# Windowed attention into a two-layer expert network: the first pair's weight splits moved to VectorE and earlier, a one-hot product moved to VectorE, a shorter unused path on ScalarE

## The chip, the cores and the metric

One core of a Trainium2 chip runs the whole program. The metric is device time in microseconds of that core, lower is better; the time shown for a kernel is the median of its runs. The engines are TensorE (PE, its weight loads PEld), VectorE (DVE), ScalarE (ACT), GpSimd (POOL) and SyncE (SP, which issues most DMAs); a "q" behind a name is that engine's instruction queue.

## The reference

```python
scores = scale * q @ k.T                     # B, H, S, D = 4, 8, 768, 64
keep = is_sink | in_window                   # 4 sinks, a window of 128
a = exp(where(keep, scores, -1e9) - max); a = a / (sum(a) + 1e-9)
x = (a @ v) as (3072, 512)
logits = x @ w_gate + modality_bias[modality_id]        # 8 experts
e_idx = argmax(logits); gate_w = softmax(logits)[e_idx]
for e in experts:
    out[e_idx == e] = gate_w * (relu(x[e_idx == e] @ w1[e]) @ w2[e])   # 512 -> 1024 -> 512
h = out @ w_in; out = (h * sigmoid(1.702 * h)) @ w_out  # 512 -> 2048 -> 512
```

All of it is float32. The kernel multiplies float32 numbers as two parts, a rounded one and the rest ("split": `exact()` writes the rounded part on ScalarE, and subtracts it from the number on a second engine, L1095 and L1096).

## The kernel before, in words

The program has four stages. **Start** (0 to 16 us): constants, the loads of the first tiles, and a branch at L1045 on whether window and sinks are of the size that the fast path handles. The path not taken, `general()`, stands in every engine's program between the branch and what follows it, so each engine jumps over its own part of it. **Attention** (to about 217 us): 24 tiles of 128 tokens. Each kind of step of a tile (`scores`, `mask`, `expo`, `ptrans`, `pevac`, `pv`, `back`, `norm` and more) has a time in the table `AT`, counted in quarters of a tile; all steps of all tiles are sorted by these times and written out in that order, which is each engine's order. The tables `OPEN` (the opening of the next stage) and `MORE` (the search for the first expert, and the loads of its weights) put further steps into the same order.

**Routing and the first pair of token blocks** (to about 257 us): the first pair's expert is chosen from the first 16 tiles, so its 256 tokens are gathered (L1016), scaled (L1116), transposed (L1107, `x0` and `x1`) and put through the expert while the attention ends. The expert's weights are 8 chunks of 512 KB (`raw0` to `raw7`, L1072 and L1073); each is split into `wah` and `wal` (128 x 1024). `first(0, f)` multiplies by chunk f's first weight (L1143, 12 matmuls, "up") and leaves relu's two parts (L1166 on ScalarE, L1169 on VectorE); `down_pair(0, f)` multiplies by its second (L1158, 12 matmuls, "down"). Beside that runs `route()`, a generator of some 45 small VectorE steps: the last tile's one-hot `pk_oh` (L649), two products on TensorE (L802, L803), then the places of all tokens, the one-hot matrices `r_es` (L908), `r_bt` (L910) and `r_at` (L914, four pieces), 24 products on TensorE (L917), and `perm` (L926), by which GpSimd gathers the second pair's tokens. The table `ADV` says how many of these steps are written inside and behind each chunk f. **The rest** (to 1091 us): 14 further pairs, single blocks, then the dense layers.

Before the change three chunks' subtractions (0, 1, 3) are VectorE's and five (2, 4, 5, 6, 7) GpSimd's (`SPLIT_V`, L982); chunks 5 to 7 are split inside the loop over f (L1231 and following), chunks 2 to 7 get their memory when the attention's value buffers are closed.

Of the kernel before, what the change touches and what calls it, by code (L numbers as in the profile page):

```python
# [17 lines left out]
P = 128  # L18
# [11 lines left out]
AT = dict(sinkevac=10.229, oevac=10.224, qevac=-2.123, kevac=-1.366, scores=-0.449, mask0=-0.2, mask1=0.21, expo0=0.692, ptrans=2.608, pevac=3.437,  # L30
          expo1=0.867, pv=7.004, qtrans=-4.358, ktrans=-1.915, back=10.991, sinktrans=9.575, norm=11.395, logits=15.779, then=16.626, pick=20.835,
          guard=5.52, invert=11.081, sinksplit=8.614)
# [3 lines left out]
OPEN = dict(split1=4.183, x0=5.146, split0=3.966, x1=5.358, split2=5.428, split3=6.826, first0=6.763, first1=6.923, split4=14.582)  # L36
MORE = 84.738, 0.617, 92.724, 1.62


def attention(tc, cst, late, first, spare, q, k, v, wg, xd, then, pick, at_tile, more, opening):  # L40
# [8 lines left out]
    with ExitStack() as ctx:  # L49
# [330 lines left out]
        def close(x, what):  # L380
            x.close()
            opening.send(what)
# [3 lines left out]
        todo.append((last("pv", "expo0", "expo1"), close, (tctx, "values")))  # L386
# [103 lines left out]
def general(tc, cst, q, k, v, wg, xd):  # L490
# [5 lines left out]
    with ExitStack() as ctx:  # L496
        per = ctx.enter_context(tc.tile_pool(name="ge1", bufs=1, side="right"))
        p2 = ctx.enter_context(tc.tile_pool(name="ge2", bufs=2, side="right"))
        ps = ctx.enter_context(tc.tile_pool(name="ge_ps", bufs=2, space=PSUM))
# [15 lines left out]
        with tc.For_i(0, B) as b, tc.For_i(0, H) as h:  # L515
# [5 lines left out]
            for nm, sc in (("q", 0.125), ("k", 1.0)):  # L521
                tr[nm] = p2.tile([D, S], F32, name=f"g_t{nm}", tag="t" + nm, bufs=1)
                for i in range(NT):
                    pt = ps.tile([P, P], F32, name=f"g_p{nm}{i}", tag="t")
                    nc.tensor.transpose(pt[0:D, :], nat[nm][:, i], ident)
                    nc.scalar.activation(out=tr[nm][:, i * P : i * P + P], in_=pt[0:D, :], func=AF.Copy, scale=sc)
            xo = p2.tile([P, NT, D], F32, name="g_x", tag="x")
            for i in range(NT):
                sc = p2.tile([P, S], F32, name=f"g_s{i}", tag="s")
                V.memset(sc, NEG)  # L530
                al = per.tile([P, S], F32, name=f"g_al{i}", tag="al")
                for g in range(2):
                    r = slice(g * 384, g * 384 + 384)
                    sp = ps.tile([P, 384], F32, name=f"g_sp{i}{g}", tag="s")
                    nc.tensor.matmul(sp, tr["q"][:, i * P : i * P + P], tr["k"][:, r], start=True, stop=True)
                    nc.scalar.activation(out=al[:, r], in_=sp, func=AF.Copy)
                V.copy_predicated(sc, keep[:, i], al)
# [8 lines left out]
                pr = p2.tile([P, NT, P], F32, name=f"g_pr{i}", tag="pr", bufs=1)  # L546
                for j in range(NT):
                    pt = ps.tile([P, P], F32, name=f"g_pp{i}{j}", tag="t")
                    nc.tensor.transpose(pt, sc[:, j * P : j * P + P], ident)
                    nc.scalar.activation(out=pr[:, j], in_=pt, func=AF.Copy)  # L550
                po = ps.tile([P, D], F32, name=f"g_po{i}", tag="o")
                for j in range(NT):
                    nc.tensor.matmul(po, pr[:, j], nat["v"][:, j], start=(j == 0), stop=(j == NT - 1))
                nc.scalar.activation(out=xo[:, i], in_=po, func=AF.Copy)
            nc.sync.dma_start(out=xv[bass.ds(b, 1), bass.ds(h, 1)].rearrange("b h p i d -> p (b h i) d"), in_=xo)
        for t in range(T):
            x = p2.tile([P, DM], F32, name=f"g_xt{t}", tag="xt")
            nc.sync.dma_start(out=x, in_=xd[t * P : t * P + P, :])
            xt = p2.tile([P, 4, P], F32, name=f"g_xT{t}", tag="xT", bufs=1)
            for c in range(4):  # L560
                pt = ps.tile([P, P], F32, name=f"g_xp{t}{c}", tag="t")
                nc.tensor.transpose(pt, x[:, c * P : c * P + P], ident)
                nc.scalar.activation(out=xt[:, c], in_=pt, func=AF.Copy)
            pl = ps.tile([P, E], F32, name=f"g_pl{t}", tag="o")
            for c in range(4):
                nc.tensor.matmul(pl, xt[:, c], wgs[:, c], start=(c == 0), stop=(c == 3))
            nc.scalar.activation(out=cst["wide"][:, t], in_=pl, func=AF.Copy)
# [221 lines left out]
def route(tc, cst, pool, tp, tot, pre, pp, perm, gates, out):  # L789
# [120 lines left out]
    nc.gpsimd.tensor_tensor(out=bt, in0=es, in1=cst["tok"].unsqueeze(2).broadcast_to([P, T, NR]), op=ALU.mult)  # L910
# [71 lines left out]
SPLIT_V = (0, 1, 3)  # L982
FIRST, SLOPE = 1, 2.0
NU = 16
ADV = [(0, 7), (4, 8), (5, 1), (12, 0), (12, 2), (11, 5)]
# [8 lines left out]
def whole(tc, q, k, v, n_sink, window, mid, wg, mb, w1, w2, w_in, w_out, out):  # L994
    nc = tc.nc
    w_in, w_out = w_in.bitcast(U32), w_out.bitcast(U32)
    with ExitStack() as ctx:
# [24 lines left out]
        with tc.manual_schedule():  # L1022
            with ExitStack() as c1:
# [33 lines left out]
                more += [(MORE[2] + MORE[3] * i, fn) for i, fn in enumerate(weights)]  # L1057
# [18 lines left out]
def layers(tc, cst, ctx, c1, m, raw, keep, perm, gates, xg, gather, load, w_in, w_out, out):  # L1076
# [10 lines left out]
    def pool(nm, stack=ctx, **kw):  # L1087
        return stack.enter_context(tc.tile_pool(name=nm, bufs=1, **near, **kw))
# [86 lines left out]
    while (what := (yield)) is not None:  # L1175
        n = int(what[-1]) if what[-1].isdigit() else 0
        if what == "scores":
# [8 lines left out]
            wa += parts(pool("wa0", side="right"), "wa", 0, 2)  # L1186
        elif what == "values":
            wa += parts(pool("wa1", side="right"), "wa", 2, CH)
        elif what[0] == "x":
            if n == 0:  # L1190
                weigh(0)
                weigh(1)
            xtrans(0, (n,))
        elif what[0] == "s":
            split(n)
        else:
            first(0, n, xt[0], 2 * P)
# [421 lines left out]
```

## Time and profile before

| | us |
|---|---|
| median of 3 runs | 1093.63 (1093.10 to 1093.99) |
| the profiled execution | 1092.52 |
| its span, first to last instruction | 1090.9 |
| TensorE busy in the span | 1058.8 (97%) |
| VectorE, ScalarE, GpSimd busy | 551.7, 406.9, 241.3 |

The profiled execution's time has 1.6 us around its span. TensorE is busy nearly throughout; the stretches where it is not lie in the first 16 us, between 217 and 262 us, and in the last 10 us. Matmuls are pipelined, so their durations overlap: matmuls of one kind follow each other by less than one lasts.

### The profile page before, as it was taken

The page shows a single profiled execution, that of the slowest core. Times are in us where ns is not written, and L with a number is a line of the kernel's source. Part 1 is how long each engine was busy: PE and PEld are TensorE (multiplying, and loading weights), DVE is VectorE, ACT ScalarE, POOL GpSimd, SP SyncE. Part 2 cuts the span into 40 slices and gives each one's busy share as a digit, 9 for nine tenths or more (in the row PEclk, how much of TensorE's full clock was granted, in tenths as well). Part 3 has the DMA queues.
Part 4 walks back from the last instruction along what each step waited for, and adds up shares of the span by engine and source line. Part 5 has one row for each costly group of instructions (what it writes and reads, how often), then busy time and mean ns, then how long its engine had stood idle before and what let it go on. Part 6 is the DMA issues. An engine that isn't in the chain of part 4 may idle for free.

```text
span 1090.9 us, 19248 instructions
## 1 busy us (share of the span) xinstructions
PE 1058.8 (97%) x6945; PEld 920.0 (84%) x6945; DVE 551.7 (51%) x1382; ACT 406.9 (37%) x979; POOL 241.3 (22%) x396
## 2 busy tenths in 40 slices
PE   7999999978999999999999999999999999999996
PEld 5787887778999999999988888888888888888885
DVE  4767768785544765422115565656533424424332
ACT  4877777643222432222223232332332323223321
POOL 2523141452333323220102222222200101101011
PEclk9999999999999999999999999999999999999999
DMA  6656555532435523125671331210203303114011
GB/s 124 137 126 138 126 122 119 139 95 77 146 113 193 158 79 99 60 81 175 192 229 39 116 109 46 97 46 32 78 1 116 115 1 116 40 76 155 1 39 39
DMA packets 172113, 108.90 MB, mean 100 GB/s; under 512 B 118000, under 2 KB 149744, under 8 KB 171984
## 3 DMA queue, kind: packets, MB, share of 16 engines
q1 hardware_dynamic: 167184, 91.62, 29.7%
q0 software_dynamic: 4800, 15.73, 4.3%
q8 instruction: 61, 1.00, 0.4%
q14 instruction: 68, 0.56, 0.2%
HBM read 79.85 MB, written 27.48 MB: 98 GB/s over the span
## 4 chain that ended last, share of the span: by engine, by line
PE 47%; issue 4%; POOL 0%; ACT 0%; POOLq 0%; DVE 0%; ACTq 0%
PE pu L1143 22%; PE pa L1150 17%; PE pu L1150 6%; PE pu L1456 1%; PE pa L1465 1%; POOL out_dram L1553 0%; POOLq L1615 0%; DVE raw L1529 0%; PE pt L1107 0%; ACT xs L1126 0%; ACT raw L1528 0%; ACT y L1467 0%; ACT ca L1458 0%; POOLq L1553 0%; ACTq L1467 0%
## 5 line engine op out<-in xcount | busy, mean ns | idle before, releaser
L1143 PE MATMUL pu<-xh,wah 128*128 128x256 f32 (+1 forms) x576 | 185.5, 322 | 0.2 <-ACT xh L1095 0.2
L1143 PE MATMUL pu<-xh,wal 128*128 128x256 f32 (+1 forms) x576 | 183.9, 319 | 0.4 <-DVEq L1252 0.4
L1143 PE MATMUL pu<-xl,wah 128*128 128x256 f32 (+1 forms) x576 | 183.9, 319 | 0.2 <-DVE xl L1096 0.2
L1529 DVE TENSOR_TENSOR raw<-pu,raw 128x512 f32<-128x512 f32 x96 | 66.3, 691 | 232.4 <-ACT raw L1528 211.7
L1528 ACT ACTIVATE raw<-pu 128x512 f32<-128x512 f32 x96 | 57.5, 599 | 291.2 <-PE pu L1143 291.2
L1158 PE MATMUL pa<-h,wah 128*128 128x256 f32 x768 | 154.8, 285 | 0.0
L1158 PEld LDWEIGHTS pa<-h,wah 128*128 128x128 f32 x768 | 127.6, 194 | 0.0
L1143 PEld LDWEIGHTS pu<-xh,wal 128*128 128x128 f32 x576 | 110.3, 192 | 8.3 <-DVEq L1252 0.6
L1143 PEld LDWEIGHTS pu<-xh,wah 128*128 128x128 f32 x576 | 110.3, 191 | 8.3 <-ACT xh L1095 0.4
L1143 PEld LDWEIGHTS pu<-xl,wah 128*128 128x128 f32 x576 | 110.2, 191 | 7.9 <-DVE xl L1096 0.4
L1158 PE MATMUL pa<-h,wal 128*128 128x256 f32 x384 | 109.2, 284 | 0.0
L1166 ACT ACTIVATE h<-pu 128x256 fp32r<-128x256 f32 x96 | 36.9, 384 | 182.5 <-PE pu L1143 182.4
L211 ACT ACTIVATE pn<-sc,mx 128x260 f32<-128x260 f32 (+1 forms) x192 | 92.8, 485 | 29.4 <-DVE mx L202 24.8
L202 DVE CUSTOM_DVE_ANT_0 sc<-s,m 128x260 f32<-128x260 f32 (+1 forms) x192 | 72.3, 396 | 48.8 <-PE s L194 43.3
L1169 DVE SCALAR_TENSOR_TENSOR h<-pu,h 128x256 fp32r<-128x256 f32 x96 | 40.4, 423 | 111.7 <-ACT h L1166 63.7
L1095 ACT ACTIVATE h<-raw 128x512 fp32r<-128x512 f32 x96 | 60.8, 634 | 77.7 <-DVE raw L1529 77.7
L1150 PE MATMUL pa<-wbh,h 128*128 128x512 f32 x216 | 76.3, 389 | 0.0
L1150 PE MATMUL pa<-wah,h 128*128 128x512 f32 x216 | 76.3, 389 | 0.0
L1143 PE MATMUL pu<-xh,wbh 128*128 128x512 f32 x192 | 74.8, 390 | 0.8 <-ACT y L1467 0.8
L1143 PE MATMUL pu<-xh,wbl 128*128 128x512 f32 x192 | 74.7, 389 | 0.0
L1143 PE MATMUL pu<-xl,wbh 128*128 128x512 f32 x192 | 74.7, 389 | 0.0
L1158 PEld LDWEIGHTS pa<-h,wal 128*128 128x128 f32 x384 | 74.4, 194 | 0.0
(322 smaller groups left out, 2036.4 us busy)
## 6 DMA issues: line engine op xcount, KB each, us to landing
raw<-in_moe_w_dram SPq DMA_DIRECT2D x64, 256.0 KB
cd<-yb SPq DMA_DIRECT2D x20, 512.0 KB
xd<-xe SPq DMA_DIRECT2D x24, 256.0 KB
raw<-yp SPq DMA_DIRECT2D x12, 512.0 KB
qn<-in_q_dram SPq DMA_DIRECT2D x22, 256.0 KB
kn<-in_k_dram SPq DMA_DIRECT2D x22, 256.0 KB
vn<-in_v_dram SPq DMA_DIRECT2D x22, 256.0 KB
yb<-y SPq DMA_DIRECT2D x10, 512.0 KB
```

What stands on the lines that cost most here:

```text
L202: nc.vector.tensor_tensor_reduce(out=sc[:, :n], in0=ps[:, :n], in1=m[:, :n], scale=1.0, scalar=3.0e38, op0=ALU.add, op1=ALU.min, accum_out=mx)
L211: nc.scalar.activation(out=pn[t][:, h, :n], in_=sc[:, :n], func=AF.Exp, scale=-1.0, bias=mx, accum_out=sums[t][:, h : h + 1])
L1095: A.activation(out=hi, in_=x, func=AF.Copy)
L1143: nc.tensor.matmul(ps[:, 0:n], w[a][:, s], cols(x, b, k), start=(k == 0 and i == 0), stop=(k == 3 and i == 2))
L1150: nc.tensor.matmul(acc, h[a][:, s], w[b][:, 512:], start=(f == 0 and j == 0), stop=(f == last and j == 2))
L1158: nc.tensor.matmul(acc[:, i % 2 * 256 : i % 2 * 256 + 256], wa[f][a][:, s], h[b], start=(f == 0 and i % 2 == 0 and j == 0), stop=(f == CH ...
L1166: A.activation(out=hi, in_=ps, func=AF.Relu)
L1169: V.scalar_tensor_tensor(out=lo, in0=ps, scalar=0.0, in1=hi.bitcast(F32), op0=ALU.max, op1=ALU.subtract)
L1456: nc.tensor.matmul(ps, raw[f][:, r], xs[s % 2][:, r], start=(k == 0), stop=(k == 3))
L1465: nc.tensor.matmul(acc[:, i * P : i * P + P], raw[f][:, 512 + i * P : 512 + i * P + P], hs[(s, f)], start=(f == 0 and i == 0), stop=(f == ...
L1528: A.activation(out=s, in_=ps, func=AF.Sigmoid, scale=1.702)
L1529: V.tensor_tensor(out=s, in0=ps, in1=s, op=ALU.mult)
```

## The change

Seven of the eight chunks are subtracted on VectorE (`SPLIT_V`), chunk 4 alone on GpSimd; all eight are split at times in `OPEN`, none in the loop, and get their memory when the attention's score buffers are closed. The loads of chunks 0 to 5 are written closer together and earlier, 7 and 6 after them. The expert search starts 2.5 quarters of a tile earlier. `r_bt` is VectorE's. The first seven steps of `route()` stand inside chunk 3 instead of behind chunk 2. `AT` has small shifts, the largest in `qtrans` (from -4.358 to -3.315). In `general()` ScalarE copies whole groups out of PSUM at once: between the branch and its end stand 63 rows of ScalarE's program where 204 stood (VectorE's 78 stay, TensorE's 198 become 80; loops of one form count once).

```diff
-AT = dict(sinkevac=10.229, oevac=10.224, qevac=-2.123, kevac=-1.366, scores=-0.449, mask0=-0.2, mask1=0.21, expo0=0.692, ptrans=2.608, pevac=3.437,
-          expo1=0.867, pv=7.004, qtrans=-4.358, ktrans=-1.915, back=10.991, sinktrans=9.575, norm=11.395, logits=15.779, then=16.626, pick=20.835,
-          guard=5.52, invert=11.081, sinksplit=8.614)
+AT = dict(sinkevac=10.41, oevac=10.141, qevac=-2.123, kevac=-1.366, scores=-0.449, mask0=0.047, mask1=0.214, expo0=0.704, ptrans=2.7, pevac=3.379,
+          expo1=0.875, pv=7.25, qtrans=-3.315, ktrans=-1.739, back=10.494, sinktrans=9.575, norm=11.26, logits=14.708, then=17.603, pick=20.992,
+          guard=5.52, invert=9.627, sinksplit=8.614)
...
-OPEN = dict(split1=4.183, x0=5.146, split0=3.966, x1=5.358, split2=5.428, split3=6.826, first0=6.763, first1=6.923, split4=14.582)
-MORE = 84.738, 0.617, 92.724, 1.62
+OPEN = dict(split1=0.538, x0=5.262, split0=3.966, x1=5.358, split2=5.498, split3=6.566, first0=6.966, first1=8.297, split4=6.709, split5=9.734, split6=10.0, split7=10.925)
+MORE = 82.223, 0.617, 91.891, 0.4, 96.0, 0.29
...
-                    pt = ps.tile([P, P], F32, name=f"g_pp{i}{j}", tag="t")
-                    nc.tensor.transpose(pt, sc[:, j * P : j * P + P], ident)
-                    nc.scalar.activation(out=pr[:, j], in_=pt, func=AF.Copy)
+                    nc.tensor.transpose(pt[:, j // 3, j % 3 * P : j % 3 * P + P], sc[:, j * P : j * P + P], ident)
+                nc.scalar.activation(out=pr.rearrange("p g j q -> p g (j q)"), in_=pt[:, :, 0 : 3 * P], func=AF.Copy)
...
-    nc.gpsimd.tensor_tensor(out=bt, in0=es, in1=cst["tok"].unsqueeze(2).broadcast_to([P, T, NR]), op=ALU.mult)
+    V.tensor_tensor(out=bt, in0=es, in1=cst["tok"].unsqueeze(2).broadcast_to([P, T, NR]), op=ALU.mult)
...
-SPLIT_V = (0, 1, 3)
+SPLIT_V = (0, 1, 2, 3, 5, 6, 7)
...
-ADV = [(0, 7), (4, 8), (5, 1), (12, 0), (12, 2), (11, 5)]
+ADV = [(0, 0), (7, 4), (8, 5), (12, 0), (12, 2), (11, 5)]
...
-                more += [(MORE[2] + MORE[3] * i, fn) for i, fn in enumerate(weights)]
+                more += [(MORE[2] + MORE[3] * i if c < 6 else MORE[4] + MORE[5] * i, weights[c]) for i, c in enumerate((0, 1, 2, 3, 4, 5, 7, 6))]
...
-            wa += parts(pool("wa0", side="right"), "wa", 0, 2)
-        elif what == "values":
-            wa += parts(pool("wa1", side="right"), "wa", 2, CH)
+            wa += parts(pool("wa", side="right"), "wa", 0, CH)
...
         down_pair(0, f - 2)
-        if f + 3 < CH:
-            split(f + 3)
         advance(ADV[f - 2][1])
```

**GpSimd, from the last tile to the second pair's gather.** `wal` is a chunk's subtraction, `r_bt` the one-hot product. Before:

```order
L305 TENSOR_TENSOR la_4746<-xe_4632 128x32
L306 TENSOR_TENSOR la_4746<-la_4746 128x16
L307 TENSOR_TENSOR lg_4745<-la_4746 128x8
L1096 TENSOR_TENSOR wal_4675<-raw_73,wah_4674 128x1024
L1096 TENSOR_TENSOR wal_4677<-raw_74,wah_4676 128x1024
L835 COPY r_num<-o_away 128x24
L1096 TENSOR_TENSOR wal_4679<-raw_75,wah_4678 128x1024
L1096 TENSOR_TENSOR wal_4681<-raw_76,wah_4680 128x1024
L910 TENSOR_TENSOR r_bt<-r_es,c_tok 128x696
```

With the change:

```order
L305 TENSOR_TENSOR la_4433<-xe_4375 128x32
L306 TENSOR_TENSOR la_4433<-la_4433 128x16
L307 TENSOR_TENSOR lg_4432<-la_4433 128x8
L1096 TENSOR_TENSOR wal_4281<-raw_73,wah_4280 128x1024
L835 COPY r_num<-o_away 128x24
L1016 DMA xg_81<-xd,perm 128x528
```

The subtractions of chunks 5 to 7 and the product are gone from here (chunk 2's stood a few rows ahead and is gone too); chunk 4's alone stands, behind GpSimd's last `lg`.

**VectorE, around the last tile's `xe` (L296, two halves) and its logits `lg`.** `pk_d` and `pk_eq` are small steps of the expert choice, which ends in `pk_oh`. Before:

```order
L296 TENSOR_TENSOR xe_4743<-bt_0_4738,rs_4598 128x288
L652 ISA pk_d,pk_mx<-lg_4745,bias 128x8
L652 ISA pk_mx 128x1
L655 SCALAR_TENSOR_TENSOR pk_eq<-pk_d,pk_mx,c_rank 128x8
L296 TENSOR_TENSOR xe_4743<-bt_1_4755,rs_4598 128x288
L309 TENSOR_REDUCE lg_4761<-xe_4743 128x8
```

With the change:

```order
L296 TENSOR_TENSOR xe_4453<-bt_1_4470,rs_4338 128x288
L652 ISA pk_d,pk_mx<-lg_4432,bias 128x8
L652 ISA pk_mx 128x1
L1096 TENSOR_TENSOR wal_4283<-raw_74,wah_4282 128x1024
L1096 TENSOR_TENSOR wal_4285<-raw_75,wah_4284 128x1024
L309 TENSOR_REDUCE lg_4482<-xe_4453 128x8
L1096 TENSOR_TENSOR wal_4287<-raw_76,wah_4286 128x1024
L655 SCALAR_TENSOR_TENSOR pk_eq<-pk_d,pk_mx,c_rank 128x8
```

Three subtractions (chunks 5, 6, 7) now stand around `lg`, in front of the last tile's choice.

**TensorE, where the routing's first two products stand.** `h` into `pa` is a down, `xh` or `xl` into `pu` an up. Before:

```order
L1158 MATMUL pa_4781<-h_4508,wah_4521 128x256
L802 LDWEIGHTS c_ones
L802 MATMUL pt_4778<-pk_oh,c_ones 128x192
L803 LDWEIGHTS c_tri
L803 MATMUL pt_4779<-pk_oh,c_tri 128x192
L1143 MATMUL pu_4515<-xh_4504,wah_4672 128x256
```

With the change:

```order
L1143 MATMUL pu_4266<-xl_4256,wah_4278 128x256
L802 LDWEIGHTS c_ones
L802 MATMUL pt_4499<-pk_oh,c_ones 128x192
L803 LDWEIGHTS c_tri
L803 MATMUL pt_4500<-pk_oh,c_tri 128x192
L1158 MATMUL pa_4501<-h_4260,wah_4274 128x256
```

The products moved from behind the down of chunk 0 to behind the up of chunk 3, which itself now stands in front of them.

## Rows read from the trace of the kernel before

**Rows 1.** Windows by stage: PE, PEld, DVE, ACT, POOL busy, PEclk, DMA share, GB/s.

```profile
30.00:200.00 170.00, 168.56 (x1585) 134.84 (x1583) 125.02 (x528) 131.12 (x442) 50.01 (x162) 1.00 0.56 124
...
228.87:233.01 4.14, 0.00 (x1) 0.00 (x0) 4.00 (x12) 0.00 (x0) 2.50 (x3) 0.97 0.10 23
233.01:244.79 11.78, 11.78 (x86) 11.57 (x85) 11.46 (x41) 3.31 (x6) 4.81 (x2) 0.87 0.12 22
244.79:250.20 5.41, 1.12 (x25) 0.91 (x25) 5.41 (x6) 0.38 (x1) 2.00 (x1) 0.96 0.00 0
250.20:257.36 7.16, 7.16 (x54) 7.16 (x52) 1.29 (x7) 1.72 (x3) 2.11 (x2) 0.79 0.26 78
```

**Rows 2.** TensorE's waits over the span: total us, times, longest.

```profile
PE qp L153 <- ACTq L1045: 5.1, 1, 5.1
PE pt L802 <- DVE pk_oh L649: 4.1, 1, 4.1
...
PE pu L1107 <- ACT xg L1116: 1.8, 1, 1.8
PE pa L917 <- DVE r_at L914: 1.6, 3, 0.6
```

**Rows 3.** The branch of L1045 by engine queue: ns, first and last start us.

```profile
L1045 ACTq COMPARE_BRANCH  x1: 73/73/73, 6.5 to 6.5; - x1
...
L1045 PEldq EVENT_SEMAPHORE  x1: 51/51/51, 7.1 to 7.1; - x1
L1045 DVEq EVENT_SEMAPHORE  x1: 21/21/21, 7.4 to 7.4; - x1
L1045 ACTq EVENT_SEMAPHORE  x1: 17/17/17, 10.5 to 10.5; - x1
```

**Rows 4.** Timeline of PE, the program's start: start us, us, instruction, [idle before].

```profile
10.54 1.12 PE L153 MATMUL qp<-ident,raw 128*128 128x128 f32 x4 [5.10 <-ACTq L1045]
...
15.55 0.71 PE L194 MATMUL s<-kts,qt 64*128 64x128 f32 x8
```

**Rows 5.** Timeline of POOL and of DVE, 226 to 243 us.

```profile
226.50 4.72 POOL L1096 TENSOR_TENSOR wal<-raw,wah 128x1024 fp32r<-128x1024 f32 x2
...
226.76 2.17 DVE L652 CUSTOM_DVE_ANT_0 pk_d<-lg,bias 128x8 f32<-128x8 f32 x1
...
228.86 2.39 DVE L655 SCALAR_TENSOR_TENSOR pk_eq<-pk_d,pk_mx,c_rank 128x8 f32<-128x8 f32 x1
...
237.86 2.38 DVE L864 TENSOR_TENSOR r_ohf<-pk_oh,r_off 128x192 f32<-128x192 bf16 x1
...
241.02 2.06 DVE L878 TENSOR_TENSOR r_w<-r_g,r_p 128x112 f32<-128x112 f32 x1
```

**Rows 6.** Groups by line and form, DVE: count, busy us, mean ns.

```profile
L1096 DVE TENSOR_TENSOR wal<-raw,wah 128x1024 fp32r<-128x1024 f32 x11 | 14.6, 1356 | 2.1 <-ACT wah L1095 2.0
...
L908 DVE TENSOR_TENSOR r_es<-r_slot,r_hi 128x696 f16<-128x696 f32 x1 | 0.9, 883 | 0.0
L842 DVE TENSOR_TENSOR r_num<-r_num,pk_oh 128x192 f32<-128x192 f32 x1 | 0.4, 351 | 0.0
```

**Rows 7.** Timeline of DVE, POOL, ACT and PE, 245 to 258 us.

```profile
245.25 4.71 DVE L914 TENSOR_TENSOR r_at<-c_npos,r_nlo 128x768 f16<-128x768 f32 x4
...
251.04 1.11 POOL L1016 DMA_INDIRECT xg<-xd,perm  x1 [3.63 <-DVE perm L926]
...
256.05 0.72 ACT L1116 ACTIVATE xg<-xg 128x512 f32<-128x512 f32 x1 [0.38 <-DMA xg<-xd,perm]
...
257.36 1.03 PE L1107 MATMUL pt<-ident,xg 128*128 128x128 f32 x8
```

**Rows 8.** Timeline of PE and ACT inside one attention tile, 142 to 147 us.

```profile
142.64 0.60 PE L153 MATMUL qp<-ident,qn 128*128 128x128 f32 x4
...
145.19 0.58 ACT L158 ACTIVATE qt<-qp 128x512 f32<-128x512 f32 x1
...
146.44 0.27 PE L247 MATMUL stp<-identr,st 128*96 128x128 f32 x1
```

More of the change, by code (lines that the diff above doesn't have):

```diff
@@ L378, in attention, with close @@
             todo.append((time, fn, (bank,)))
-        def close(x, what):
+        def close(x, what=None):
             x.close()
-            opening.send(what)
+            if what:
+                opening.send(what)
         last = lambda *names: 4 * T + 0.01 + max(AT[nm] - kinds[nm][0] for nm in names)
         todo.append((last("scores", "mask0", "mask1"), close, (sctx, "scores")))
-        todo.append((last("pv", "expo0", "expo1"), close, (tctx, "values")))
+        todo.append((last("pv", "expo0", "expo1"), close, (tctx,)))
         for nm, time in OPEN.items():
@@ L498, in general @@
         p2 = ctx.enter_context(tc.tile_pool(name="ge2", bufs=2, side="right"))
-        ps = ctx.enter_context(tc.tile_pool(name="ge_ps", bufs=2, space=PSUM))
+        ps = ctx.enter_context(tc.tile_pool(name="ge_ps", bufs=1, space=PSUM))
         wgs = per.tile([P, 4, E], F32, name="g_wg")
@@ L521, in general @@
             for nm, sc in (("q", 0.125), ("k", 1.0)):
-                tr[nm] = p2.tile([D, S], F32, name=f"g_t{nm}", tag="t" + nm, bufs=1)
+                tr[nm] = p2.tile([D, 2, 3 * P], F32, name=f"g_t{nm}", tag="t" + nm, bufs=1)
+                pt = ps.tile([P, 2, 512], F32, name=f"g_p{nm}", tag="t")
                 for i in range(NT):
-                    pt = ps.tile([P, P], F32, name=f"g_p{nm}{i}", tag="t")
-                    nc.tensor.transpose(pt[0:D, :], nat[nm][:, i], ident)
-                    nc.scalar.activation(out=tr[nm][:, i * P : i * P + P], in_=pt[0:D, :], func=AF.Copy, scale=sc)
+                    nc.tensor.transpose(pt[0:D, i // 3, i % 3 * P : i % 3 * P + P], nat[nm][:, i], ident)
+                nc.scalar.activation(out=tr[nm], in_=pt[0:D, :, 0 : 3 * P], func=AF.Copy, scale=sc)
             xo = p2.tile([P, NT, D], F32, name="g_x", tag="x")
@@ L530, in general @@
                 V.memset(sc, NEG)
-                al = per.tile([P, S], F32, name=f"g_al{i}", tag="al")
+                al = per.tile([P, 2, 3 * P], F32, name=f"g_al{i}", tag="al")
+                sp = ps.tile([P, 2, 512], F32, name=f"g_sp{i}", tag="s")
                 for g in range(2):
[L533 to L537, printed above, removed]
+                    nc.tensor.matmul(sp[:, g, 0 : 3 * P], tr["q"][:, i // 3, i % 3 * P : i % 3 * P + P], tr["k"][:, g], start=True, stop=True)
+                nc.scalar.activation(out=al, in_=sp[:, :, 0 : 3 * P], func=AF.Copy)
+                V.copy_predicated(sc, keep[:, i], al.rearrange("p g k -> p (g k)"))
                 mx = p2.tile([P, 1], F32, name=f"g_m{i}", tag="m")
@@ L559, in general @@
             xt = p2.tile([P, 4, P], F32, name=f"g_xT{t}", tag="xT", bufs=1)
+            pt = ps.tile([P, 4, P], F32, name=f"g_xp{t}", tag="x")
             for c in range(4):
[L561 to L564, printed above, removed]
+                nc.tensor.transpose(pt[:, c], x[:, c * P : c * P + P], ident)
+            nc.scalar.activation(out=xt, in_=pt, func=AF.Copy)
             for c in range(4):
-                nc.tensor.matmul(pl, xt[:, c], wgs[:, c], start=(c == 0), stop=(c == 3))
-            nc.scalar.activation(out=cst["wide"][:, t], in_=pl, func=AF.Copy)
+                nc.tensor.matmul(pl[:, t], xt[:, c], wgs[:, c], start=(c == 0), stop=(c == 3))
+        nc.scalar.activation(out=cst["wide"], in_=pl, func=AF.Copy)
 NP = 15
```

6 lines of the change are left out of this document (4 added, 2 removed).

## Prediction

> **What bounds the kernel now.** I read the windows by stage first, then TensorE's waits, then the timelines around the few waits that are left. In the attention TensorE is busy 168.56 of 170 us, so a re-ordering there can give back at most 1.4 us; after 262 us no wait of TensorE's is longer than 0.9 us until the last 10 us, so whatever is won or lost before 262 us arrives whole at the end. Its real waits are these [rows 2]: 5.1 us at the start for ScalarE's queue, 1.8 us for the first pair's tokens, 4.1 us for `pk_oh` (the window from 228.87 us on holds no matmul at all), and 4.3 us out of 5.41 at the one-hot product [rows 1]. TensorE's clock stands at full rate but for two stretches: the mean of 0.87 over 11.78 us and of 0.79 over 7.16 us [rows 1] are each some 1.5 us of work lost, 0.13 x 11.78 and 0.21 x 7.16, and each follows a wait of 4 us or more.
>
> **The start.** ScalarE compares at 6.5 us like the others, and its next instruction runs at 10.5 us; VectorE's runs at 7.4 us [rows 3]. ScalarE does nothing else in these 4 us, so I read them as the fetch of the code behind a far jump. The first transposes wait for it until 10.54 us [rows 4]. The change takes ScalarE's jump from 204 rows to 63, fewer than VectorE's 78. So I put ScalarE at 7.4 us and TensorE's start with it: **-3.1 us**. Bounds: 0, if any jump of ScalarE costs 4 us, and -3.4, down to TensorE's own 7.1 us. What comes next can follow: the first scores start 5.0 us behind the transposes [rows 4], with filler matmuls of fixed number between, so all of it moves with the start.
>
> The trace's reading meets a rule that speaks against it. The Trainium skill ("Runtime: NRT & Kernel Launch", Instruction fetch mechanics) says that an engine holds two blocks of 256 instructions each, and that only a jump out of both has to wait for a fetch. By that rule a jump of 204 rows would not have stalled, and a shorter one would save nothing; the sum would then be that of the first rival.
>
> **The attention's order.** The work is the same, and TensorE is full. In the change the next tile's query transpose stands one product later, and its PSUM bank is taken again by the fourth probability transpose, no longer by the sink transpose. Before, the bank's copy ends at 145.77 us and its next user starts at 146.44 us, 0.67 us later [rows 8]. I take 0; bounds -1.4 us (all idle time gone) and +3 us (0.13 us more for each of 23 tiles, if the 0.67 us are just overdrawn).
>
> **The first pair's start.** The gather is written 2.5 quarters of a tile earlier, so the 1.8 us for `xg` go. In their place TensorE waits at the last tile's first `back`, which the change puts in front of chunk 0's up, for ScalarE: there a split of chunk 2 stands ahead of the copies that `back` needs. A wait of about 2 us in front of the up, but with one `back` done in it: I take **-0.6 us** (bounds -1.8 and +1).
>
> **From the last tile to `pk_oh`.** Before, GpSimd subtracts two chunks from 226.50 to 231.2 us, and in that time two VectorE steps of 8 elements last 2.17 and 2.39 us [rows 5], where one of 192 elements lasts 0.351 us elsewhere [rows 6]: some 4.2 us are lost on the way to `pk_oh`. What this shows is that a VectorE step with two SBUF inputs stands still while GpSimd works. With the change, three subtractions stand on VectorE in that place, 3 x 1.356 = 4.1 us [rows 6]. So nothing is won here: **-0.1 us**. Bounds: -4.2 (the three wait for nothing and fit where VectorE idled) and +4.1 (the 4.2 us were idle time anyway). The wait for `pk_oh` gets another cover: an up of 12 matmuls moves in front of the first product. TensorE waits some 1.4 us less there and has as much less to do later.
>
> **The routing.** Two steps lie under GpSimd's other two subtractions: `r_ohf` with 2.38 us and `r_w` with 2.06 us [rows 5]. A step of the same 192 elements beside an idle GpSimd lasts 0.351 us [rows 6]. Both subtractions are gone: -2.03 and -1.71. The one-hot product costs VectorE about what `r_es` of the same size does, +0.88 us [rows 6]; but on GpSimd it lay beside the first `r_at`, and the four took 4.71 us [rows 7], while TensorE's three waits between them, 1.6 us [rows 2], with 0.28 us of matmuls after each (1.12 us in four batches, [rows 1]) put the undisturbed ones 0.8 to 0.9 us apart: 4 x 0.87 = 3.5, so -1.2. One relu step of 0.4 us now stands ahead of the last `r_at`. Sum: **-3.7 us** (bounds -4.1, and 0 if the long steps are long by themselves).
>
> The Trainium skill ("SBUF — State Buffer", Who interferes with whom) states the cause: VectorE and GpSimd share a port pair that one holds for a whole instruction, and a VectorE step with two SBUF inputs contends with GpSimd's reads. It cuts both ways: by that rule the moved subtractions now hold up GpSimd's small steps. That would matter where TensorE waits for those; the wait is in the second rival's price.
>
> **The second pair's tokens.** From the gather's first issue at 251.04 us over the second's landing at 256.05 and its scaling to 256.77 us the transposes could start at about 256.9 us; they started at 257.36 us [rows 7], because TensorE still had cover. With the change only two downs of 1.44 us (seven such groups fill the 11.78 us less the lost clock and the products, [rows 1]) are left behind the one-hot product, where before there were four groups. So TensorE follows the gather: **-0.5 us**, but it stands idle for 3 to 3.7 us right before, and like after the waits of 4 us the clock may fall behind it, this time without cover: **+1.5 us** (bounds 0 and 1.6).
>
> **Sum.** -3.1 - 0.6 - 0.1 - 3.7 - 0.5 + 1.5 = -6.5 us. The profiled execution's 1092.52 us (its span is 1090.9) becomes 1086.0; it stands 1.1 us under the median, so against the median of 1093.63 us I predict **1087.1 us**. Bounds of the single terms do not add up in one direction; -3.4 at the start, no fallen clock and 1 us from the order give 1084.
>
> **The rivals.** *The start stays as it is*: the 4 us are no matter of distance. For it: TensorE jumps over nearly as many rows as ScalarE and is back at 7.1 us [rows 3]. Against it: ScalarE alone is held, and nothing else runs there. Then 1087.1 + 3.1 = 1090.2 us. This is also what the skill's two-block rule would give. *VectorE takes GpSimd's place*: the 4.1 us of subtractions in front of `pk_oh` come on top, because the steps that were held had nobody waiting, or because chunk 4's subtraction and the small GpSimd steps now collide with those on VectorE. For it: VectorE is busy 4.00 of the 4.14 us in which TensorE waits [rows 1]. Then 1087.1 + 4.2 = 1091.3 us. *The new order stalls the attention*: the fourth probability transpose comes 3.2 us behind the query transpose, and the copy between them ended 3.13 us behind it before [rows 8]; if each tile waits 0.5 us there, 22 tiles cost 11 us, and the time is 1098 us. It decides from about 0.4 us a tile; below that the gains win. For it: the slack that was 0.67 us is all but gone. Against it: TensorE's own transpose work moves later with it, and ScalarE is idle a quarter of the time.
>
> **How the numbers follow.** The forecast has 0.58, the start that stays 0.19, VectorE in GpSimd's place 0.15, the stalling order 0.08. A measurement here can tell about 0.2%, 2.2 us, from no change. The forecast and the first rival lie below 1091.4 us, and the second at that bound: faster 0.85, within 0.2% 0.09, slower 0.06. The range goes from 1083.8 (the good ends above) to 1091.4 us (the second rival) and leaves out the third.
>
> **What would show it.** Right: ScalarE's first instruction behind the branch near 7.4 us and the first transposes there; `r_ohf` and `r_w` under 0.5 us; TensorE's wait at the one-hot product nearly gone, and a new one of 3 us before the second pair's transposes, with a lower clock behind it. Wrong: ScalarE still at 10.5 us; a new wait of TensorE in every tile; `pk_oh` later than 233 us less the start's gain.

## The result and the profile after

The changed kernel takes 1078.13 us (median of four runs, 1077.19 to 1079.94) against 1093.81 us of the kernel before on the same chip (four runs, 1093.1 to 1094.4): a ratio of 0.9862, with a 95% interval of 0.985 to 0.9874. That is 15.7 us faster. The direction was forecast, the size was not: the forecast was 6.5 us, and the time lies below the range.

The profiled execution has a span of 1075.9 us, 15.0 us shorter than before. A table of when TensorE reaches the same points says where the 15.0 us lie. Each number is the time between the starts of two rows of TensorE's timeline: the first and the last group of scores (L194), the first pair's token transposes (L1107), the product with `pk_oh` (L802), the first and the last batch of the one-hot product (L917), the second pair's transposes (L1107) and the end of the span. The other rows of the table belong to experiments and are used there.

| kernel | first scores at | to the last scores | to the first pair's tokens | to `pk_oh`'s product | to the one-hot product | one-hot product | to the second pair's tokens | to the end |
|---|---|---|---|---|---|---|---|---|
| before | 15.55 | 189.39 | 12.56 | 15.51 | 14.45 | 2.56 | 7.34 | 833.54 |
| after | 10.46 | 185.19 | 12.23 | 13.14 | 10.12 | 2.94 | 7.45 | 834.37 |
| start alone | 12.33 | 189.37 | 12.83 | 15.99 | 14.58 | 2.55 | 7.49 | 834.36 |
| order alone | 15.10 | 183.06 | 12.05 | 19.94 | 14.66 | 2.55 | 8.48 | 833.76 |
| end alone | 15.77 | 190.75 | 12.79 | 13.81 | 10.34 | 2.74 | 7.48 | 833.82 |
| change without its start | 15.20 | 183.21 | 12.21 | 13.16 | 10.11 | 2.93 | 7.28 | 833.60 |
| change without its order | 12.11 | 191.35 | 12.64 | 13.82 | 11.49 | 2.53 | 6.22 | 834.24 |
| change, splits on GpSimd | 11.90 | 183.20 | 12.22 | 17.61 | 10.31 | 2.75 | 7.48 | 834.13 |
| order, first up moved | 14.95 | 183.07 | 12.04 | 17.14 | 14.24 | 2.56 | 8.52 | 834.98 |
| before, longer warming | 12.30 | 189.39 | 12.56 | 16.61 | 14.57 | 2.56 | 7.95 | 834.56 |

From before to after: 5.1 us at the start, 4.2 in the attention, 0.3 on the way to the first pair's tokens, 2.4 up to `pk_oh`, 4.3 in the routing, and 1.3 us given back behind it (0.38, 0.11 and 0.83). The attention was forecast at nothing.

TensorE's waits after the change, which answer to [rows 2] (total us, times, longest):

```profile
PE pa L917 <- DVE r_at L914: 3.1, 4, 1.1
...
PE bt L275 <- ACT stt L252: 2.0, 1, 2.0
PE qp L153 <- PEq L1045: 1.8, 1, 1.8
PE pt L802 <- DVE pk_oh L649: 1.2, 1, 1.2
```

The 5.1 us for ScalarE's queue have become 1.8 us for TensorE's own, the 4.1 us for `pk_oh` are 1.2, the one-hot product waits 3.1 us (4.3 before: to the 1.6 us of [rows 2] comes the row below, which [rows 2] leaves out), and the 1.8 us for the first pair's tokens are now 2.0 us for the copy `stt` of the last tile. Before:

```profile
PE pa L917 <- POOL r_bt L910: 2.7, 1, 2.7
```

The branch by queue, against [rows 3]: ScalarE is back at 6.9 us, 3.6 us earlier.

```profile
L1045 ACTq COMPARE_BRANCH  x1: 73/73/73, 6.4 to 6.4; - x1
...
L1045 ACTq EVENT_SEMAPHORE  x1: 17/17/17, 6.9 to 6.9; - x1
...
L1045 PEldq EVENT_SEMAPHORE  x1: 51/51/51, 7.0 to 7.0; - x1
```

VectorE's timeline in the end, against [rows 5]: three subtractions in place of the held steps, and `r_ohf` and `r_w` short.

```profile
216.24 2.36 DVE L1096 TENSOR_TENSOR wal<-raw,wah 128x1024 fp32r<-128x1024 f32 x2
...
218.71 1.21 DVE L1096 TENSOR_TENSOR wal<-raw,wah 128x1024 fp32r<-128x1024 f32 x1
...
220.66 0.31 DVE L649 TENSOR_TENSOR pk_oh<-pk_eq,pk_best 128x32 bf16<-128x32 f32 x1
...
225.65 0.35 DVE L864 TENSOR_TENSOR r_ohf<-pk_oh,r_off 128x192 f32<-128x192 bf16 x1
...
227.12 0.26 DVE L878 TENSOR_TENSOR r_w<-r_g,r_p 128x112 f32<-128x112 f32 x1
```

And twelve half tiles in the middle of the attention, from the start of the 18th group of scores to that of the 30th, in a window of each trace (us, busy time of PE, PEld, DVE, ACT, POOL with counts, granted clock). Before:

```profile
78.43:128.19 49.76, 49.63 (x470) 39.78 (x468) 35.20 (x151) 38.58 (x131) 13.17 (x45) 1.00 0.57 129
```

After:

```profile
73.25:120.96 47.71, 47.71 (x470) 39.18 (x469) 35.17 (x152) 37.26 (x131) 13.19 (x46) 1.00 0.60 134
```

The same 470 matmuls at the same granted clock were "busy" for 49.63 of 49.76 us and are busy for 47.71 of 47.71 us. So the busy time of before held some 2 us in 50 that were no work. What they were shows in the weight loads (PEld) around one back product. Before:

```profile
143.29 0.14 PEld L220 LDWEIGHTS pt<-ident,pn 128*128 128x128 f32 x1
143.64 0.54 PEld L278 LDWEIGHTS bt<-btw,oh 128*128 128x128 f32 x4 [0.21 <-ACT pn L211]
```

After:

```profile
134.70 0.14 PEld L220 LDWEIGHTS pt<-ident,pn 128*128 128x128 f32 x1
134.81 0.55 PEld L278 LDWEIGHTS bt<-btw,oh 128*128 128x128 f32 x4
```

Loads that wait for nothing follow one another by 0.11 us. Before, the back product's came 0.35 us behind the last transpose's. The transpose's own matmul row lasts 0.27 us by its modelled end, and covers the gap, so that no wait of TensorE shows. The trace puts the wait down to ScalarE's `pn`, which is no input of the back product (`btw` and `oh` are); a run with another PSUM bank, below, asks whether it was the bank.

### The profile page after: what moved, and what is told of

Its sections match the earlier page's. It is cut to its first block, busy times and chain, and to the rows that moved or that the text cites. A ratio compares the mean times of both kernels' runs of the same rounds, so it can differ in the third digit from the quotient of the medians.

```text
span 1075.9 us, 19234 instructions
## 1 busy us (share of the span) xinstructions
PE 1050.3 (98%) x6945; PEld 915.8 (85%) x6945; DVE 547.3 (51%) x1387; ACT 402.4 (37%) x979; POOL 228.7 (21%) x391
## 4 chain that ended last, share of the span: by engine, by line
PE 48%; issue 4%; POOL 0%; ACT 0%; POOLq 0%; DVE 0%; ACTq 0%
PE pu L1143 23%; PE pa L1150 17%; PE pu L1150 6%; PE pu L1452 1%; PE pa L1461 1%; POOL out_dram L1549 0%; POOLq L1611 0%; DVE raw L1525 0%; PE pt L1107 0%; ACT xs L1126 0%; ACT raw L1524 0%; ACT ca L1454 0%; POOLq L1549 0%; ACTq L1524 0%; ACTq L1454 0%
## 5 line engine op out<-in xcount | busy, mean ns | idle before, releaser
L211 ACT ACTIVATE pn<-sc,mx 128x260 f32<-128x260 f32 (+1 forms) x192 | 92.5, 484 | 17.4 <-DVE mx L202 13.1
L202 DVE CUSTOM_DVE_ANT_0 sc<-s,m 128x260 f32<-128x260 f32 (+1 forms) x192 | 70.0, 400 | 37.3 <-PE s L194 35.8
```

What stands on the lines that cost most here:

```text
L202: nc.vector.tensor_tensor_reduce(out=sc[:, :n], in0=ps[:, :n], in1=m[:, :n], scale=1.0, scalar=3.0e38, op0=ALU.add, op1=ALU.min, accum_out=mx)
L211: nc.scalar.activation(out=pn[t][:, h, :n], in_=sc[:, :n], func=AF.Exp, scale=-1.0, bias=mx, accum_out=sums[t][:, h : h + 1])
```

## The experiments: the parts alone

Sixteen kernels ran. All compute the same as before; what differs is where a step stands, on which engine, in which bank, or how far a jump goes.

**The start alone.** The kernel before with the changed `general`, which is not run here and only jumped over:

```
-        ps = ctx.enter_context(tc.tile_pool(name="ge_ps", bufs=2, space=PSUM))
+        ps = ctx.enter_context(tc.tile_pool(name="ge_ps", bufs=1, space=PSUM))
...
-                    nc.scalar.activation(out=pr[:, j], in_=pt, func=AF.Copy)
+                nc.scalar.activation(out=pr.rearrange("p g j q -> p g (j q)"), in_=pt[:, :, 0 : 3 * P], func=AF.Copy)
...
```

> The kernel before with the shorter general path alone; nothing that runs in this case changes but the distance of the jump over it. Theory A (ScalarE's jump is 3.1 to 3.3 us shorter, and the wait that is left is short enough for TensorE to keep the full clock, which is worth another 1.8 us on the transposes and the fillers): first scores near 10.5 us of the span, time 1088.7 us. Theory B (the prediction's: only the jump): first scores near 12.4 us, 1090.7 us. Theory C (the distance is no matter): 1093.8 us.

1091.3 us, ratio 0.9987 (0.9978 to 0.9997): 1.4 us by the ratio. The transposes start at 7.26 us, 3.3 us earlier than in the profile before, so the 4 us of [rows 3] hung on the distance of the jump, and Theory C falls. The first scores came at 12.33 us, Theory B's value, but of these 3.2 us only a part arrives at the end: by the table 1.0 us is given back up to the second pair's tokens and 0.8 us behind them, where the kernels differ by up to 1.5 us anyway (833.5 to 835.0).

**The order alone.** The kernel before with the changed `AT`:

```
-AT = dict(... ptrans=2.608, ... qtrans=-4.358, ... back=10.991, ...
+AT = dict(... ptrans=2.7, ... qtrans=-3.315, ... back=10.494, ...
```

> The kernel before with the new numbers of the attention's table alone. Theory A (the back product stood behind the fourth transpose of its half tile and waited there for a PSUM bank that VectorE was still copying; in the new place it does not): a half tile of the middle tiles takes 4.13 us instead of 4.29 and 3.75 instead of 3.93, together some 4 us or more over the attention, time near 1089.5 us, with TensorE's busy share no lower than before. Theory B (TensorE was full, as the prediction had it, and the attention got faster by something else in the change, such as earlier loads): half tiles as before, 1093.8 us.

1091.77 us, 0.9986 (0.9975 to 0.9998). In the trace Theory A: the half tiles take 4.13 and 3.75 us instead of 4.29 and 3.93, and the attention is 6.3 us shorter. But 4.4 us of it are gone before `pk_oh`'s product, 19.94 us from the first pair's tokens instead of 15.51. The last tile's first back product now stands in front of the first up, and waits there with nothing to cover it; TensorE's timeline:

```profile
210.21 0.33 PE L1107 MATMUL pu<-ident,xg 128*128 128x128 f32 x1 [0.80 <-ACT xg L1116]
...
217.48 0.41 PE L275 MATMUL bt<-svb,stt 96*128 96x288 f32 x1 [1.96 <-ACT stt L252]
...
230.15 0.34 PE L802 MATMUL pt<-pk_oh,c_ones 128*128 128x192 bf16 x1 [3.03 <-DVE pk_oh L649]
```

The window of this stage shows the clock as well, a mean of 0.81 where before it had 0.99:

```profile
210.21:230.15 19.94, 13.01 (x84) 11.53 (x84) 11.00 (x24) 7.57 (x13) 9.21 (x11) 0.81 0.46 131
```

**The end alone.** The kernel before with the rest: `OPEN`, `MORE`, the order of the weights' loads, one pool for all parts, and

```
-    nc.gpsimd.tensor_tensor(out=bt, in0=es, ...
+    V.tensor_tensor(out=bt, in0=es, ...
...
-SPLIT_V = (0, 1, 3)
+SPLIT_V = (0, 1, 2, 3, 5, 6, 7)
...
-ADV = [(0, 7), (4, 8), (5, 1), (12, 0), (12, 2), (11, 5)]
+ADV = [(0, 0), (7, 4), (8, 5), (12, 0), (12, 2), (11, 5)]
...
-        if f + 3 < CH:
-            split(f + 3)
```

> The kernel before with all of the change but the shorter general path and the attention's table: the weights' places, the splits on VectorE, the one-hot product on VectorE, the routing's steps. Theory A (three gains that do not touch each other): the end's 5.7 us alone, 1088.1 us. Theory B (the end's gain was sized rightly at 3.4 us and what is more comes from the attention's order): 1090.4 us. Under both r_ohf and r_w take under 0.4 us.

1087.67 us, 0.9953 (0.9936 to 0.9969), 5.1 us: Theory A. The three parts alone make 1.4 + 1.5 + 5.1 = 8.0 us of the 15.1 that the ratio of the whole gives.

## The experiments: the parts taken out

**Without its start.** The changed kernel with the old `general`.

> The changed kernel with the long general path of before: the change without its start. Alone the start gave 2.0 us (1091.3 against 1093.3), of which its profile shows 3.2 us at the first scores, with 1.8 us given back behind the attention. Theory A (the parts need each other: with the waits of the end gone, nothing is given back): slower than the changed kernel by 3.2 us for the jump, or by 5.1 us if the clock at the start hangs on the jump as well: 1081.4 to 1083.3 us. Theory B (each part is worth what it gave alone): 1080.1 us.

1080.09 us, 0.988 (0.9864 to 0.9897): Theory B's value. The start is worth 2.0 us within the change (0.9880 - 0.9862 = 0.0018 of the time), about what it gave alone. The two intervals leave this difference uncertain by some 2 us, so that the whole 3.1 us of the forecast is not excluded here. Order and end together give 13.1 us, where alone they gave 1.5 and 5.1: it is these two that need each other.

**Without its order.** The changed kernel with the old `AT`.

> The changed kernel with the attention's table of before: start and end without the order. Alone the order gave 1.5 us, though its profile shows the attention 6.3 us shorter. Theory A (behind the change's end the 6.3 us arrive, less about 2 us of new waits in the last tiles): slower than the changed kernel by 4 to 6 us, 1082 to 1084 us. Theory B (worth the 1.5 us that it gave alone): 1079.6 us.

1085.96 us, 0.9934 (0.9918 to 0.9951): more than either theory. By the ratios the order is worth 7.9 us within the change. The table shows 6.2 us of it in the attention against the profile of after, whose attention had waits of 2 us in its first tiles (below), and 8.1 us against the profiles of the change without its start and with the splits on GpSimd (183.2): 6.2 us in the steady tiles, 0.6 us in waits of this profile's first tiles, and 1.4 us in the last six half tiles, which the end's steps lengthen with the old numbers.

## The experiments: what makes the order faster

**The back product alone.**

```
-AT = dict(... back=10.991, ...
+AT = dict(... back=10.494, ...
```

> The kernel before with one number of the attention's table changed: the back product goes one transpose group ahead (in the half tile with the query transpose the order is then pt, query, back, pt; in the change it is pt, back, query, pt). Theory A (the bank that the back product waits for): most of the order's gain, half tiles near 4.13 to 4.2 us, 1089.5 to 1091 us. Theory B (it is the query transpose's later place, or several numbers together): half tiles stay at 4.29 us, 1093.8 us.

In the trace Theory A without a rest: half tiles of 4.13 and 3.75 us, 183.13 us of attention. The time is 1090.38 us (0.9981, 0.9971 to 0.9991), for the same reason as with the order alone: it waits 2.05 us for `stt` in front of the ups.

**Another bank.**

```
-NS_BUFS = 4
-NT_BUFS = 3
+NS_BUFS = 3
+NT_BUFS = 4
```

> The kernel before, its attention's order unchanged, with four PSUM banks for transposes and back products instead of three, and three for scores instead of four (there are eight in all). Theory A (the back product waits in each half tile for the bank that VectorE's copy of the transpose three before it still holds): the weights of the back product are loaded 0.1 us behind the last transpose's instead of 0.35, in every half tile, while the scores now wait for their three banks, which may cost more than it gives: no time is predicted. Theory B (it is not the bank): the gap in front of the back product stays.

With four banks the old order has no gap in front of the back product; weight loads, in the old order:

```profile
154.78 0.14 PEld L220 LDWEIGHTS pt<-ident,pn 128*128 128x128 f32 x1
154.89 0.55 PEld L278 LDWEIGHTS bt<-btw,oh 128*128 128x128 f32 x4
```

VectorE's copy of the transposes of this half tile, before and here:

```profile
142.84 0.69 DVE L231 COPY pts<-pt 128x512 f32<-128x512 f32 x1
```

```profile
154.33 0.69 DVE L231 COPY pts<-pt 128x512 f32<-128x512 f32 x1 [1.03 <-PE pt L220]
```

Before, it ended at 143.53 us and the load came at 143.64; here it runs until 155.02 us, and the load at 154.89 did not wait for it. So it is the bank. The price is as feared: the scores wait for their three banks, 4.95 us a half tile and 1128.08 us in one run. Three banks are enough if the product stands where its bank has long been copied, which is what the change does.

## The experiments: the end

**The splits back on GpSimd.**

```
-SPLIT_V = (0, 1, 2, 3, 5, 6, 7)
+SPLIT_V = (0, 1, 3)
```

> The changed kernel with the lower parts of chunks 2, 5, 6 and 7 subtracted on GpSimd again (chunks 0, 1 and 3 on VectorE as before). Theory A (GpSimd's long instructions hold up VectorE's steps with two inputs in SBUF, as in the rows of before): VectorE steps of 0.2 to 0.4 us again last 2 us and more while GpSimd subtracts, the first-pair choice pk_oh and the one-hot product come later, slower by 2 to 6 us, 1080 to 1084 us. Theory B (the prediction's: on VectorE the subtractions cost in front of pk_oh what the held steps cost): pk_oh comes as late as in the changed kernel, and only the routing's part differs, 1078 to 1080 us.

1081.32 us, 0.9898 (0.9881 to 0.9914): 3.9 us slower by the ratios, Theory A. VectorE's and GpSimd's timelines of this kernel:

```profile
217.40 2.30 DVE L655 SCALAR_TENSOR_TENSOR pk_eq<-pk_d,pk_mx,c_rank 128x8 f32<-128x8 f32 x1
219.61 2.40 DVE L652 CUSTOM_DVE_ANT_0 pk_d<-lg,bias 128x8 f32<-128x8 f32 x1
...
222.06 2.25 DVE L655 SCALAR_TENSOR_TENSOR pk_eq<-pk_d,pk_mx,c_rank 128x8 f32<-128x8 f32 x1
```

```profile
217.24 7.05 POOL L1096 TENSOR_TENSOR wal<-raw,wah 128x1024 fp32r<-128x1024 f32 x3 [0.61 <-ACT wah L1095]
```

GpSimd's row is three subtractions of 2.35 us each, and beside them three VectorE steps of 8 elements last as long. Where GpSimd is quiet these steps take 0.22, 0.16 and 0.23 us, so 6.3 us are lost; on VectorE the same three cost 3.6 us. `r_ohf` and `r_w` stay at 0.35 and 0.26 us, as nothing is left for GpSimd there. This is what the Trainium skill says in "SBUF — State Buffer" (Who interferes with whom), of the port pair that one of the two engines holds for a whole instruction; the trace agrees, with 2.25 to 2.40 us against 2.35.

**The one-hot product back on GpSimd.**

```
-    V.tensor_tensor(out=bt, in0=es, ...
+    nc.gpsimd.tensor_tensor(out=bt, in0=es, ...
```

> The changed kernel with the one-hot product r_bt on GpSimd again, beside the first of the four r_at. Theory A (the prediction's: 1.2 us for it, since beside it VectorE's first r_at is held): slower by about 1.2 us, 1079.3 us, the wait at the product led by GpSimd again. Theory B (VectorE's own 0.88 us cost as much as they save): no difference, 1078.1 us.

1079.49 us, 0.9869 (0.9851 to 0.9886), which can't be told from the changed kernel, so that the time decides for neither theory. From `pk_oh`'s product to the last batch it takes 10.40 + 2.89 us, in the change 10.12 + 2.94. VectorE's first three `r_at` last 3.85 us beside GpSimd's product. In the change they last 2.69 us, but the product itself, now VectorE's, takes 0.88 us. So the 1.2 us are there in the `r_at`, and the product's own time takes back most of them.

**Earlier back products in the changed kernel.** Two numbers of `OPEN`, one at a time and together.

```
-OPEN = dict(... split2=5.498, ...
+OPEN = dict(... split2=6.45, ...
...
-OPEN = dict(... first0=6.966, ...
+OPEN = dict(... first0=6.45, ...
```

> The changed kernel with one number changed: ScalarE's half of chunk 2's split goes behind the sink copy stt that the last tile's first back product waits for (2.05 us in the changed kernel; the split's copy of 1.06 us stands ahead of stt there). Theory A (the wait is ScalarE's queue, and pk_oh follows the back products): the wait falls to 1.0 us and all behind it comes 1.0 us earlier, 1077.1 us against the changed kernel's 1078.1. Theory B (VectorE's steps to pk_oh and the routing set the end of this stage, whatever TensorE does ahead of them): TensorE waits 1 us more at pk_oh instead, 1078.1 us.

> The changed kernel with one number changed: the first pair's first up goes in front of the last tile's first back product, as in the kernel before, so that it lies in the 2.05 us for stt. Theory A: the wait is covered by the up's 1.44 us, the second back product comes some 0.9 us earlier, 1077.2 us. Theory B (VectorE sets the end of the stage): pk_oh at the same distance from the last scores and a longer wait for it, 1078.1 us.

> The last two together. Theory A: the wait for stt is gone or under 0.3 us, pk_oh 1 to 1.5 us earlier, 1076.6 us. Theory B: 1078.1 us.

1077.65 us (0.9856, 0.984 to 0.9872), 1077.24 us (0.9854, 0.9837 to 0.987) and 1078.1 us (0.9858, 0.9842 to 0.9874): none can be told from the changed kernel. The waits for `stt` fell to 1.1 us, nothing and nothing; those for `pk_oh` rose from 1.2 to 2.0, 2.3 and 2.3. Theory B: VectorE's steps set the time of `pk_oh`.

**Less on VectorE.** Chunk 7's split leaves `OPEN` and stands in front of its up.

```
-..., split6=10.0, split7=10.925)
+..., split6=10.0)
     for f in range(2, CH):
+        if f == CH - 1:
+            split(f)
         first(0, f, xt[0], 2 * P, ...
```

> The changed kernel with chunk 7's split written behind the routing, in front of its own up, instead of within the last tile's steps: VectorE's subtraction of 1.2 us leaves the path to pk_oh and the one-hot product, and lies where VectorE idles. Theory A (VectorE's queue sets this stage): pk_oh and the one-hot product 1.0 to 1.2 us earlier behind the last scores, 1077.0 us against 1078.1. Theory B (the choice waits for the back products, and the subtraction lies beside that): no change, 1078.1 us.

> The last one with the first up in front of the back product as well. Theory A: pk_oh another 0.5 to 1 us earlier, since with less on VectorE the earlier back products count, 1076.2 us. Theory B: 1077 to 1078 us.

1077.48 us (0.9857, 0.9843 to 0.9871) and 1078.39 us (0.9864, 0.9849 to 0.9878). In the trace of the first `pk_oh`'s product comes 1.1 us earlier (12.02 us behind the first pair's tokens instead of 13.14), and so does the one-hot product: VectorE's queue is the bound there, as Theory A has it. With the first up moved as well it comes at 12.44 us, 0.4 us later again and not earlier as that run's Theory A had it. In the time nothing of it can be seen. From the one-hot product to the second pair's tokens it took 8.12 us instead of 7.45, and the window from the first batch to the tokens has a mean clock of 0.69, where the change has 0.84 (231.14 to 241.53 us):

```profile
229.78:240.84 11.06, 9.10 (x73) 8.80 (x73) 5.37 (x11) 1.91 (x4) 2.11 (x2) 0.69 0.16 50
```

That the fallen clock took the rest was not tested by itself. No version here is shown to beat the change.

## The experiments: what was still open

**The order with the first up where it was.** The order alone, and in the old `OPEN` `first0=6.45` for 6.763, so that the up again stands in front of the back product.

> The kernel before with the new attention's table (as in the run of the order alone, 1091.8 us) and one number of the end's table more: the first pair's first up goes in front of the last tile's first back product, where it stood before. Theory A (the 6.3 us that the order gave were lost because the back product now stood in front of the ups and waited 2 us for ScalarE with nothing to cover it, and the clock fell behind it): most comes through, 1088 to 1089.5 us. Theory B (VectorE and GpSimd, with the subtractions that hold each other up, set the time of pk_oh, whatever TensorE does ahead of it): 1091 to 1092 us, with the wait for pk_oh longer by what the back product waits less.

1087.99 us, 0.995 (0.9938 to 0.9962): Theory A. One number in the end's table brings the order from 1.5 to 5.5 us. To `pk_oh`'s product it is 17.14 us instead of 19.94, at a mean clock of 0.90 instead of 0.81. The remaining 1.6 us to the 15.51 of before were not taken apart.

**A busy TensorE at the start.**

```
-WARM = 13
+WARM = 28
```

> The kernel before with 28 warming matmuls ahead of the branch instead of 13, so that TensorE works until about 8.9 us and waits less than 2 us for its own jump, instead of 5.1 us for ScalarE's. Theory A (what the wait costs at the start is also the clock behind it, 1.8 us on transposes and fillers): first scores near 13.8 us instead of 15.5, and the time 0 to 1.8 us shorter, 1091.5 to 1093.3 us. Theory B (the clock at the start is no matter of that wait): first scores at 15.1 to 15.8 us as in the other runs with the long jump, 1093.3 us.

Neither theory as it stood: the scores came earlier than A's value, the time is B's. TensorE's timeline of the start:

```profile
2.49 5.32 PE L413 MATMUL warm_o<-raw 128*128 128x256 bf16 x28 [2.49 <-POOL raw L409]
9.09 0.66 PE L153 MATMUL qp<-ident,raw 128*128 128x128 f32 x4 [1.28 <-ACTq L1045]
...
12.30 0.72 PE L194 MATMUL s<-kts,qt 64*128 64x128 f32 x8
```

The transposes ran at the full rate (0.66 us for four, 1.12 in [rows 4]), the 20 fillers behind them too (2.35 us, 3.31 before), and the transposes started 1.4 us earlier than in the profile before, so the first scores came 3.2 us earlier. The 1.4 us need not be the warming's: ScalarE is back at 9.0 us here, and at 9.0 to 10.5 us in the eight kernels with the long path. The time is 1093.48 us, 1.0002 (0.9992 to 1.0011): nothing arrived. In the table the 3.2 us go behind the attention, 1.1 on the way to `pk_oh`, 0.6 at the second pair's tokens and 1.0 in the rest.

## Why the prediction was wrong

**The bound.** "In the attention TensorE is busy 168.56 of 170 us, so a re-ordering there can give back at most 1.4 us" is the step that failed, and with it the term of 0 for the order. The runs show 6.3 us in the attention, for the back product's new place alone, and 7.9 us within the change. The reading of [rows 1] took busy time for work. A transpose's row lasts 0.27 us where the next can start 0.11 us later, so a wait of less than about 0.16 us hides under it; here one lay in almost every half tile. The argument did look at the turn of the PSUM banks, but at the query transpose's bank and its 0.67 us [rows 8], and not at the product that waited. The rival built on it, a stalling order, fell with it: no half tile of the steady tiles is longer than before.

**The start.** The mechanism was right: with 63 rows to jump over, ScalarE is back at 6.9 us, forecast 7.4, and the transposes start at 7.25 to 7.50 us in all ten kernels with the short path, against 9.09 to 10.54 us in the eight with the long one. The two-block rule of the Trainium skill ("Runtime: NRT & Kernel Launch", Instruction fetch mechanics), by which a jump of 204 rows would not have stalled, does not fit these rows, if a row is taken for one instruction. The size was off. The profile before happened to show the longest of the eight long ways back: 4.0 us from ScalarE's compare to its next instruction, where the others show 2.5 to 3.5 us. And "all of it moves with the start" holds up to the first scores, but at the end 1.4 us arrive alone (0.3 to 2.4 by its interval) and 2.0 within the change. The profile of after flatters the start by 1.4 to 1.9 us: its first scores come at 10.46 us, because both the transposes (four in 0.63 us) and the 20 fillers (2.35 us) ran at the full rate, as in four of the ten kernels; the other six have them at 11.9 to 12.4 us. One of these six, the start alone, had the transposes at the full rate too, but its fillers took 4.01 us, with a granted clock of 0.57 from 8.39 to 12.33 us. The profile of after loses 2 us again in the 7th, 8th and 10th half tile (4.62, 4.73 and 5.13 us instead of 4.13, 4.13 and 4.26), and the last scores are at 195.65 us, where two kernels with the same order and the late start have 195.10 and 195.59. But the early start is not shown to cause these waits: the kernel with `split2=6.45` and the one with both numbers start late (12.35 and 12.00 us), have such waits as well, and reach the last scores at 196.66 and 196.85 us.

**The first pair's start, -0.6 us.** The wait for `stt` came as described, 2.05 us for ScalarE behind a split, and the 1.8 us for `xg` went. Both lie behind the first of the tokens' transposes, so the table's 0.3 us is not the whole: from the last scores to the last back product (L278 at 225.26 us before, 214.81 after) it takes 19.16 us instead of 20.32. That is 1.2 us less, within the bounds.

**From the last tile to `pk_oh`, -0.1 us.** From that back product to `pk_oh`'s product it takes 6.21 us instead of 7.75: 1.5 us less, within the bounds. The two prices were about right: the three subtractions cost 3.6 us (forecast 4.1) where the held steps lost 4.2. That makes 0.6 us; besides, the second half of `xe`, which stood behind the held steps (0.45 us at 231.17), now lies ahead of the subtractions, and the remaining half microsecond was not taken apart. What the step did not see is that the new order changes the comparison: with GpSimd's subtractions in it, three steps are held, not two, for 6.3 us. That VectorE's subtractions hold up GpSimd's small steps in turn can be seen too (L241 and L242 last 1.24 and 1.19 us at 201.65 and 205.19, and 0.25 and 0.21 us elsewhere), but TensorE waits only 0.3 us for it.

**The routing, -3.7 us.** Measured -4.33 up to the product and +0.38 in it, together -3.95. `r_ohf` and `r_w` gave 2.03 and 1.80 us, as forecast. The product's three terms came about as written: the first three `r_at` are 1.16 us shorter than beside GpSimd's product, the product takes 0.88 us and the relu step 0.42. Their sum was forecast at +0.1 us; -0.1 us is what the measured sum leaves for it.

**The second pair's tokens, -0.5 and +1.5 us.** Wrong, by a miscount: not two downs lie behind the one-hot product but three and an up, as many groups as before, so TensorE had cover and did not wait, and the transposes come 7.45 us behind the product instead of 7.34. The clock did fall, but ahead of that, behind the four batches: the window from 234.25 to 237.50 us has 0.50, about as before.

**What the sum missed as a sum.** The parts were priced one by one, and they are not worth the same alone. That what is won before 262 us "arrives whole at the end" held to within 1.5 us only: behind the second pair's tokens the kernels of the table take 833.5 to 835.0 us. The order's gain is time on TensorE ahead of a stage that VectorE, ScalarE and GpSimd set. With the old end it runs into that stage's waits, and the clock falls behind them; with the new end it comes through.

## What to carry to other kernels

Do not bound what a re-ordering can give by TensorE's busy share: compare start-to-start times of a repeated piece, and look in the weight loads for one that comes later than its neighbours, then ask whose bank it needs and who still reads it. When a stage behind is timed by a table of its own, move that table with the stage ahead, or the gain turns into waits and a lower clock; test parts in pairs, not only alone. Keep long GpSimd instructions out of stretches in which short VectorE steps with two SBUF inputs are on the path.

## What was not expected of the hardware

- The way back from the same long jump of ScalarE lets the transposes start between 9.09 and 10.54 us, in eight kernels in which that path is the same code; with the short one they start between 7.25 and 7.50 us.
- With the same code up to that point and the same wait (1.80 to 2.05 us), TensorE's first transposes ran at the full rate in five executions (four in 0.63 us) and at about half of it in five others (1.08 or 1.09 us). The granted clock does not tell them apart: it reads 1.00 over these transposes in the profile of after, which has the fast ones, and 1.00 in that of the kernel with both numbers, which has the slow ones.
- Time saved early is not always time saved: 3.2 us at the first scores gave nothing with the longer warming (1.0002), 1.4 us with the start alone. What in the end takes it back, beyond the waits and the clock that the rows show, is not settled.
